# Rows of six experts gathered by quarters of channels and turned by VectorE instead of TensorE

## The chip, the cores and the metric

The kernel runs on one core of a Trainium2 chip. The metric is the time of one execution on the device in microseconds, the median of several executions.

## The reference

A windowed attention (4 batches, 8 heads, 768 positions, 64 channels a head; each query sees the first 8 keys and the last 96) gives 3072 tokens x of 512 channels. A router sends each token to the one expert of eight whose embedding is nearest by cosine, and the expert's output is scaled by the router's probability:

```python
logits = xn @ en.T / tau
expert_idx = np.argmax(logits, axis=1)
...
for e in range(E):
    mask = expert_idx == e
    h = np.maximum(x[mask] @ w1[e], 0.0)           # 512 -> 1024
    out[mask] = gate_w[mask, None] * (h @ w2[e])   # 1024 -> 512
```

All is in fp32. Each expert has 2 MB of w1 and 2 MB of w2. TensorE sums over the 128 partitions, so x must lie with its channels on the partitions (xT) ahead of the first product, while a gather brings tokens onto the partitions (xg).

## The kernel before

The first 200 us are attention and routing; x is written to DRAM (x_dram, one row of 2 KB a token), and so are, for each expert, the numbers of its tokens and their gates (meta, loaded into mt; idss holds the numbers as integers). Then the experts follow one another, each in two parts.

- The arm, one of several code paths by the count w of the expert's tokens (here 320, 512, 320, 352, 384, 480 and 384 for experts 1 to 7), held in a Switch that TensorE, ScalarE (ACT) and VectorE (DVE) enter by a branch. In it `first_by_seven` makes h by Strassen's scheme: seven products of 16 matmuls (L1312) in place of eight, with sums of blocks of w1 (fsum, and one in the place of a block of w1 itself: L1079 to L1082) and of xT (xsum: L1054 to L1057) as operands. The names of these sum lines are shared: `right_sums` and `left_sums` serve several operands, so the operand names tell them apart. After most products `plus` (L1324) adds them up on VectorE, and `fill` then calls a list of pending sums. At the end come the sums of h (hsum) and the rows beyond the first 256 tokens (L1245 for whole tiles of 128, L1258 for pieces of 64 and 32).
- The pair, for the first 256 tokens: seven products again (L1117), with sums of w2 (wsum) and of h. `Pair.begin` and `Pair.end` hold them; `begin` also calls three lists of pending sums.

The sums and the turned rows that expert e+1 needs are made during expert e. `between`, called after each product of the arm, lets TensorE turn one tile of 128 rows of expert e+1 by four transposes (`turn_row`, L1026), and ACT copies the two halves into xT (L1029). In xT the tokens are laced: 16 of one half, 16 of the other. `expert` deals the pending sums to the lists: in the arm the sums of w2, then two of w1 of the next expert, then two of xT; in the pair the other two of xT, then the other two of w1.

The order on every engine is the order of the program text. On POOL, for each e: the gathers of expert e+1 (`gather_rows`, L1000, four of 128 whole rows), then the scatters of the results of expert e-1 (L1264), then a drain. POOL does not enter the arms and so runs ahead: rows of an expert are gathered about a stage before they are turned. On SP's queue, `load_weights` issues w1 of expert e+1 (L167) behind the first product of the pair of expert e-1, and w2 (L168) behind that pair; for expert 2 both wait for the last scatter of expert 0 and come at the start of expert 1. Buffers: two each of w1, w2 and xT, eight tiles xg, four banks for the products.

Of the kernel before, what the change touches and what calls it, by code (L numbers as in the profile page):

```python
# [9 lines left out]
F32 = mybir.dt.float32  # L10
# [10 lines left out]
P = 128  # L21
# [2 lines left out]
PIECES = 32  # L24
FIRST = 256
LACE = 16
WIDTHS = [128] + list(range(160, CAP + 1, 32))
PAIR = WIDTHS.index(256)

# [134 lines left out]

def load_weights(k, e, w):
    nc = k.nc
    first = nc.sync.dma_start(w[0][:], k.w1[e].rearrange("(c p) f -> p c f", p=P))  # L167
    nc.sync.dma_start(w[1][:], k.w2[e].rearrange("(f p) m -> p f m", p=P))  # L168
    return first

# [824 lines left out]
def gather_rows(k, ids, xgp, NJ=CAP // P, upto=None):  # L995

    xgs, issued = [], []
    for j in range(NJ):
        xg = xgp.tile([P, k.DM], F32, name="xg", tag="xg")
        i = k.nc.gpsimd.indirect_dma_start(  # L1000
            out=xg[:], out_offset=None, in_=k.x_dram[0 : upto or k.N + 1, :],
            in_offset=bass.IndirectOffsetOnAxis(ap=ids[:, j, 0:1], axis=0),
        )
        xgs.append(xg)
        issued.append(i.ins)
    return xgs, issued


def new_turned(k):
    return k.xtp.tile([P, k.NC, 2, CAP // 2], F32, name="xT", tag="xT")  # L1010

# [280 lines left out]
            between(f)  # L1292


def first_by_seven(k, now, hT, w, between, spare):


    nc, h = k.nc, w // 2
    a = first_weights(k, now.w[0])
    b = [[now.xT[:, 2 * i : 2 * i + 2, j] for j in range(2)] for i in range(2)]  # L1300
    s1, s2, s3, s4 = now.first_sums
    t1, t2, t3, t4 = now.token_sums
    out = [[laced(hT[:, 4 * i : 4 * i + 4, 0:w])[:, j] for j in range(2)] for i in range(2)]
    number = [0]

    def banks():
        return [k.big.tile([P, CAP], F32, name="big", tag="big") for _ in range(2)]

    def product(to, x, y, add=False):
        for f in range(4):  # L1310
            for l in range(2):
                nc.tensor.matmul(to[f // 2][:, f % 2 * 256 : f % 2 * 256 + h], lhsT=x[:, l, f * P : (f + 1) * P], rhs=y[:, l, 0:h],  # L1312
                                 start=not (add or f % 2 or l), stop=True, skip_group_check=True)
        between(number[0])
        number[0] += 1

    def pairs(ps, q):
        for i in range(2):
            x = ps[i][:].rearrange("p (f n) -> p f n", f=2)[:, :, 0:h].rearrange("p f (q i) -> p f q i", i=LACE)
            yield x, q[:, 2 * i : 2 * i + 2]  # L1320

    def plus(ps, z, q, last=False):
        for (x, to), (_, z) in zip(pairs(ps, q), pairs(ps, z)):
            nc.vector.tensor_tensor(out=to, in0=x, in1=z, op=ALU.add)  # L1324
            if last:
                nc.scalar.activation(to, to, AF.Relu)  # L1326
        fill()

    def fill():
        for make in spare.pop(0):  # L1330
            make()

    (q11, q12), (q21, q22) = out
    fill()
    x, y = banks(), banks()
    product(x, a[0][0], b[0][0])
    for ps, q in pairs(x, q21):
        nc.scalar.copy(out=q, in_=ps)
    product(y, s2, t2)
    plus(y, q21, q12)  # L1340
    product(x, a[0][1], b[1][0], True)
    for ps, q in pairs(x, q11):
        nc.scalar.activation(q, ps, AF.Relu)
    product(y, s3, t3, True)
    plus(y, q21, q22)
    v = banks()
    product(v, s1, t1)
    plus(v, q22, q22, True)
    product(y, a[1][1], t4, True)
    plus(y, q21, q21, True)  # L1350
    product(v, s4, b[1][1], True)
    plus(v, q12, q12, True)


def expert(k, now, coming, widths, unfinished):


    tc = k.tc
    w1, w2 = now.w
    hT = new_hidden(k)  # L1360
    if coming:
        coming.xT = new_turned(k)

    def between(f):
        at = {1: (0,), 2: (1,), 3: (2,), 4: (3,)} if now.e else {5: (0,), 6: (1, 2), 7: (3,)}
        for j in at.get(f, ()) if coming else ():
            turn_row(k, coming.rows, coming.xT, j, k.nc.scalar.copy)

    a = [[hT[:, 4 * j : 4 * j + 4, i * P : (i + 1) * P] for j in range(2)] for i in range(2)]
    now.sums, spare = weight_sums(k, w2)  # L1370
    left, making = hidden_sums(k, a)
    more, ahead = [], []
    if coming:
        coming.token_sums, more = token_sums(k, coming.xT)
        if now.e:
            coming.first_sums, ahead = first_sums(k, coming.w[0])
    spare = [spare[:2], spare[2:], ahead[:1], ahead[1:2], more[:2], []]
    if now.e == 1:
        spare[2:6] = [], ahead[:1], ahead[1:2] + more[:1], more[1:2]
    tiles = range(2 if now.e else 1, CAP // P)  # L1380
    ps = None if now.e else k.work0.tile([P, k.DM], F32, name="work", tag="work")
    k.order = list(range(4, 8)) + list(range(4)) if now.e else list(range(8))
    steps = widths_of(now.e)
    for arm in tc.Switch(now.width.index, len(steps), hint=now.width.hint):
        w = steps[arm]
        if now.e:
            first_by_seven(k, now, hT, w, between, list(spare))
            for make in making:
                make()
        else:  # L1390
            first_by_eight(k, now.xT, w1, hT, w, between)
        for size in (32, 64):
            if w % (2 * size) >= size:
                part_in_arm(k, now, hT, w2, w // (2 * size) * 2 * size, size)
        for j in tiles:
            if j < w // P:
                second_in_arm(k, now, hT, w2, j)
        if ps:
            second(k, ps, hT, w2, range(k.NF // 2))

    def scatters():
        for j in tiles:
            scatter_rows(k, now.y[:, j - 1, :], now.tile_ids[:, j : j + 1])
        for size in (64, 32):
            scatter_rows(k, now.y_part[size][:], now.parts[size][0], P // size)

    def choose_next():
        if coming:
            give_hint(k, coming.e, widths[coming.e])

    out = [scatters]
    if now.e:
        pair = Pair(k, now.rows, a, left, w2, now.sums, not coming)
        choose_next()
        out += unfinished.pop()()
        number = [lambda: widths.append(take_width(k, now.e + 2))] if now.e + 2 < k.E else []
        if now.e == k.E - 2:
            number.append(lambda: load_flag(k))
        if now.e == 2:
            ahead.append(lambda: flag_leftover(k))  # L1420
        pair.begin(spare=(more[2:], number + ahead[2:3], ahead[3:]))
        ps = k.work0.tile([P, k.DM], F32, name="work", tag="work")
        unfinished.append(pair.end(ps[:, 0:256]))
        out.append(pair.scatter(1))
    else:
        choose_next()
        widths.append(take_width(k, 2))
        out += unfinished.pop()()
        for make in more:
            make()  # L1430
        second(k, ps, hT, w2, range(k.NF // 2, k.NF))
        unfinished.append(lambda: end_second(k, now.rows, ps))
    return out
# [172 lines left out]
def kernel(  # L1606
# [40 lines left out]
    with ExitStack() as moe:  # L1647
# [43 lines left out]
        def prepare(e):  # L1691
            t = Net()
            t.e = e
            t.y, t.y_part = ys[e % 2]
            xgs, t.gathers = gather_rows(n, n.ids[:, e], n.xgp)
            t.rows = n.mt[:, e], n.ids[:, e], xgs
            if e < 2:
                t.w = n.w[e]
            else:
                t.w = new_weights(n, (wp_a, n.wp_b)[e % 2])  # L1700
            return t

        with tc.manual_schedule(engines=ORDERED | set(ARMS) | {mybir.EngineType.Pool}):
# [26 lines left out]
            for j in range(CAP // P):  # L1730
                turn_row(n, coming.rows, coming.xT, j, nc.vector.tensor_copy)
            cast(2, n.E)
            split_rows(n, n.mt)
            for y, parts in ys:
                for x in (y, *parts.values()):
# [5 lines left out]
            for e in range(n.E):  # L1741
                now, coming = coming, None
                parts_of(n, now)
                now.width = widths[e]
                if e == 1:
                    now.first_sums = first
                if e + 1 < n.E:
                    coming = prepare(e + 1)
                for scatter in pending:
                    scatter()  # L1750
                if e and coming:
                    wait_for(n, load_weights(n, e + 1, coming.w), [n.outs[-1] if e == 1 else n.out_again])

                nc.gpsimd.drain()
                pending = expert(n, now, coming, widths, unfinished)
# [33 lines left out]
```

## Time and profile before

| | us |
|---|---|
| median of 3 runs (521.31 to 528.96) | 526.16 |
| the profiled execution | 523.85 |
| its span | 522.0 |
| TensorE (PE) busy | 500.9 |
| VectorE (DVE) busy | 301.3 |
| ScalarE (ACT) busy | 197.4 |
| GpSimd (POOL) busy | 148.7 |

The arms of experts 1 to 7 begin at 234.18, 268.58, 320.97, 353.83, 390.62, 429.60 and 479.00 us of the span, their pairs at 254.94, 308.48, 341.55, 377.78, 417.30, 466.80 and 504.10 us.

A line of the timeline gives start, duration (of a run of equal instructions together), engine, line of the kernel, operation, output and inputs with their sizes and the count. A line of the chain of waits gives start, duration and what the chain went through. A line of the table by windows gives the window, its length, the busy time of PE, its weight loads, DVE, ACT and POOL with their counts of instructions, the clock granted to TensorE, the mean busy share of the 16 DMA engines and the GB/s they moved. A group's line gives line, engine, operation, operands and count, then busy us and mean ns of one, then idle time ahead of it and what ended that. "PE x <- y: a, b, c" is a us of waiting in b waits, the longest c.

### The profile page before, as it was taken

How to read it: one execution, taken by the hardware profiler on the slowest of the kernel's cores; microseconds unless marked ns; L12 is line 12 of the kernel's file. 1: busy time of each engine (PE TensorE's matmuls, PEld its weight loads, DVE VectorE, ACT ScalarE, POOL GpSimd, SP SyncE). 2: the span in 40 equal slices, each digit the busy share in tenths (PEclk: the TensorE clock that was granted, in tenths of full speed). 3: DMA queues.
4: the chain of work that ended last, by engine and by line, in shares of the span. 5: the costliest groups of instructions: out<-in, count | busy, mean ns of one | idle time of the engine just before them, and what ended most of it. 6: DMA issues, size and time to landing. Idle time of an engine off the chain costs nothing.

```text
span 522.0 us, 13698 instructions
## 1 busy us (share of the span) xinstructions
PE 500.9 (96%) x5606; PEld 412.8 (79%) x5606; DVE 301.3 (58%) x602; ACT 197.4 (38%) x493; POOL 148.7 (28%) x169
## 2 busy tenths in 40 slices
PE   8999999999987998899989999999999999999995
PEld 7777787787765687859878659989889789859964
DVE  5646667766774664846745606765646644715531
ACT  4966776777644311303222312412312222302210
POOL 4221121432443326253340024153053050013023
PEclk9999999999998999999999999999999999999999
DMA  8989999998524336818682018457066065001001
GB/s 166 202 174 182 220 238 217 222 232 204 131 69 121 104 62 143 251 46 290 207 287 99 2 50 285 156 198 263 3 217 242 4 224 164 1 15 68 0 22 67
DMA packets 111421, 76.32 MB, mean 146 GB/s; under 512 B 87077, under 2 KB 95269, under 8 KB 111281
## 3 DMA queue, kind: packets, MB, share of 16 engines
q1 hardware_dynamic: 102769, 59.00, 42.6%
q0 software_dynamic: 6912, 15.26, 8.7%
q8 instruction: 63, 1.03, 0.9%
q14 instruction: 77, 0.63, 0.5%
q10 hardware_dynamic: 1600, 0.39, 0.3%
HBM read 61.66 MB, written 17.16 MB: 151 GB/s over the span
## 4 chain that ended last, share of the span: by engine, by line
PE 64%; issue 24%; POOL 5%; DVE 3%; ACT 2%; POOLq 1%; DMA 1%; DVEq 0%
PE big L1312 15%; PE big L1117 8%; PE od L512 7%; PE pa L483 6%; PE pa L458 4%; PE work L1258 3%; PE od L522 3%; PE pa L681 3%; PE work L1117 3%; POOL out_dram L1264 3%; PE work L1245 3%; PE work L1026 2%; PE big L1288 2%; PE pa L585 2%; PE work L1036 1%
## 5 line engine op out<-in xcount | busy, mean ns | idle before, releaser
L496 DVE TENSOR_TENSOR ex<-ex,table 126x768 f32<-126x768 f32 x64 | 60.3, 947 | 41.4 <-ACT ex L489 38.5
L1324 DVE TENSOR_TENSOR hT<-big,hT 128x320 f32<-128x320 f32 (+4 forms) x70 | 39.4, 566 | 49.2 <-PE big L1312 46.8
L1264 POOL DMA_INDIRECT out_dram<-y_arm,tids x17 | 17.0, 1002 | 170.4 <-ACT y_arm L1247 121.3
L489 ACT ACTIVATE ex<-pa 126x384 f32<-126x384 f32 (+1 forms) x128 | 53.7, 476 | 24.0 <-PE pa L483 17.7
L1312 PE MATMUL big<-xT,w1t 128*128 128x160 f32 (+4 forms) x336 | 59.4, 330 | 1.3 <-issue 1.3
L1312 PEld LDWEIGHTS big<-xT,w1t 128*128 128x128 f32 x336 | 54.2, 190 | 4.0 <-issue 2.2
L512 PE MATMUL od<-ex,v 126*64 126x192 f32 (+1 forms) x576 | 46.8, 309 | 0.0
L1000 POOL DMA_INDIRECT xg<-x_dram,idss x32 | 32.3, 1011 | 43.9 <-PE big L1312 21.7
L483 PE MATMUL pa<-qT,kT 64*32 64x128 f32 (+3 forms) x2048 | 40.8, 268 | 2.8 <-issue 2.5
L483 PEld LDWEIGHTS pa<-qT,kT 64*32 64x32 f32 (+1 forms) x2048 | 30.5, 107 | 15.2 <-issue 10.6
L512 PEld LDWEIGHTS od<-ex,v 126*64 126x64 f32 x576 | 35.2, 138 | 7.7 <-issue 3.5
L259 POOL DMA_INDIRECT meta<-mt,slot x24 | 27.4, 1141 | 43.8 <-DVE rd L556 17.8
L1312 PE MATMUL big<-xsum,fsum 128*128 128x160 f32 (+4 forms) x224 | 39.6, 330 | 0.0
L1029 ACT COPY xT<-work 128x256 f32<-128x256 f32 x56 | 18.0, 377 | 56.7 <-PE work L1026 55.3
L1312 PEld LDWEIGHTS big<-xsum,fsum 128*128 128x128 f32 x224 | 36.1, 190 | 1.1
L1245 PE MATMUL work<-w2t,hT 128*128 128x512 f32 x80 | 35.1, 593 | 0.0
L1117 PE MATMUL big<-wsum,hsum 128*128 128x256 f32 x136 | 31.1, 380 | 1.5 <-issue 1.0
L1326 ACT ACTIVATE hT<-hT 128x320 f32<-128x320 f32 (+4 forms) x42 | 21.6, 533 | 25.5 <-DVE hT L1324 25.3
L433 POOL COPY v<-v 30x896 f32<-30x896 f32 (+1 forms) x15 | 16.6, 1119 | 49.0 <-DMA v<-in_v_dram 30.5
L1117 PEld LDWEIGHTS big<-wsum,hsum 128*128 128x128 f32 x136 | 25.7, 190 | 6.0 <-issue 1.8
L1245 PEld LDWEIGHTS work<-w2t,hT 128*128 128x128 f32 x80 | 15.1, 190 | 17.7 <-issue 17.6
L1122 DVE TENSOR_TENSOR ptmp<-big,ptmp 128x256 f32<-128x256 f32 x16 | 6.7, 421 | 37.6 <-PE big L1117 16.9
(246 smaller groups left out, 903.0 us busy)
## 6 DMA issues: line engine op xcount, KB each, us to landing
w1t<-in_moe_w_dram SPq DMA_DIRECT2D x6, 2048.0 KB
w2t<-in_moe_w_dram SPq DMA_DIRECT2D x6, 2048.0 KB
v<-in_v_dram SPq DMA_DIRECT2D x32, 192.0 KB
x_dram<-xs SPq DMA_DIRECT2D x23, 256.0 KB
k<-in_k_dram SPq DMA_DIRECT2D x28, 192.0 KB
q<-in_q_dram SPq DMA_DIRECT2D x28, 192.0 KB
w1t<-in_moe_w_dram SPq DMA_DIRECT2D x32, 128.0 KB
w2t<-in_moe_w_dram SPq DMA_DIRECT2D x32, 128.0 KB
```

The costliest lines, as they stand in the source:

```text
L259: i = nc.gpsimd.indirect_dma_start(out=k.meta[:], out_offset=bass.IndirectOffsetOnAxis(ap=slot[:, t : t + 1], axis=0), in_=mt[:, t, :], in ...
L483: i = nc.tensor.matmul(u.sp[e][k0:k1, a * n + c0 : a * n + c1], lhsT=t.kT[rows, j, k0:k1], rhs=t.qT[rows, j * BLK + c0 : j * BLK + c1], st ...
L489: nc.scalar.activation(u.ex[:, e], u.sp[e][0:ROWS, 0 : 2 * u.n].rearrange("p (a c) -> p a c", a=2), AF.Exp, scale=k.scale)
L496: nc.vector.tensor_tensor(out=exv, in0=exv, in1=tab[:, :, 0 : u.n // BLK, :], op=ALU.mult)
L512: nc.tensor.matmul(g.od[a][e * D : (e + 1) * D, at : at + c1 - c0], lhsT=g.v[0:ROWS, 2 * a + e, u.j, :], rhs=u.ex[:, e, a, c0:c1], start=f ...
L1000: i = k.nc.gpsimd.indirect_dma_start(out=xg[:], out_offset=None, in_=k.x_dram[0 : upto or k.N + 1, :], in_offset=bass.IndirectOffsetOnAxis ...
L1117: i = self.k.nc.tensor.matmul(ps, lhsT=x[:, f, :], rhs=w[:, f, :], start=f == 0 and not add, stop=True, skip_group_check=True)
L1245: nc.tensor.matmul(ps[:], lhsT=hT[:, f, j * P : (j + 1) * P], rhs=w2[:, f, :], start=i == 0, stop=i == k.NF - 1)
L1264: i = k.nc.gpsimd.indirect_dma_start(out=k.out.rearrange("t (i m) -> (t i) m", i=n), out_offset=bass.IndirectOffsetOnAxis(ap=ids, axis=0), ...
L1312: nc.tensor.matmul(to[f // 2][:, f % 2 * 256 : f % 2 * 256 + h], lhsT=x[:, l, f * P : (f + 1) * P], rhs=y[:, l, 0:h], start=not (add or f ...
L1324: nc.vector.tensor_tensor(out=to, in0=x, in1=z, op=ALU.add)
L1326: nc.scalar.activation(to, to, AF.Relu)
```

## The change

Experts 2 to 7 get their turned rows another way.

- `gather_quarters`: a tile of 128 tokens is gathered by four indirect DMAs instead of one. Partition 32 b + r of DMA g receives quarter b (128 channels, 512 bytes) of token 32 g + r. The row numbers for it, four times the token's number plus b, are made once for all six experts by `square_rows`, in 16 small VectorE instructions.
- `turn_squares`: one VectorE transpose of 128x512, which turns each square of 32x32 by itself, writes the tile into xT, laced as before. Channels then lie on the partitions as 128 b + 32 c + j on partition 32 b + j, chunk c.
- So w1 of these experts is loaded with its rows in that order, by four DMAs, one for each chunk c.
- `between` stays for expert 0 alone. In experts 1 to 6 the turns take the places in the arm at which two sums of xT stood (one turn in expert 1, two in the others); the others are called at the first place in the pair, all four sums of xT at the second, and the last two sums of w1 at the third.
- Of expert 2, six quarter gathers are issued ahead of the scatters of expert 0, where four whole gathers were, and ten behind them. For the others all 16 stand where the four stood.

```diff
 def load_weights(k, e, w):
-    first = nc.sync.dma_start(w[0][:], k.w1[e].rearrange("(c p) f -> p c f", p=P))
+    src = k.w1[e].rearrange("(b c j) f -> c b j f", b=4, j=SQ)
+    first = [nc.sync.dma_start(w[0][:, c, :], src[c]) for c in range(k.NC)][0]
     nc.sync.dma_start(w[1][:], k.w2[e].rearrange("(f p) m -> p f m", p=P))
...
+def square_rows(k):
+    k.squares = k.tp.tile([P, k.E, CAP // P, 4], I32, name="squares")
+    for b in range(4):
+        for g in range(4):
+            k.nc.vector.tensor_scalar(out=k.squares[b * SQ : (b + 1) * SQ, 2:, :, g], in0=k.mt[g * SQ : (g + 1) * SQ, 2:, :, 0],
+                                      scalar1=4.0, scalar2=float(b), op0=ALU.mult, op1=ALU.add)
+
+def gather_quarters(k, ids, xgs, lo, hi):
+    src = k.x_dram[:, :].rearrange("t (b c) -> (t b) c", b=4)
+    for i in range(lo, hi):
+        j, g = divmod(i, 4)
+        k.nc.gpsimd.indirect_dma_start(
+            out=xgs[j][:, g * P : (g + 1) * P], out_offset=None, in_=src,
+            in_offset=bass.IndirectOffsetOnAxis(ap=ids[:, j, g : g + 1], axis=0),
+        )
+
+def turn_squares(k, xgs, xT, j):
+    half = P // 2
+    k.nc.vector.transpose(
+        out=xT[:, :, :, j * half : (j + 1) * half].rearrange("p c a (g i) -> p g c a i", i=LACE),
+        in_=xgs[j][:].rearrange("p (g c r) -> p g c r", g=4, r=SQ),
+    )
...
     def between(f):
-        at = {1: (0,), 2: (1,), 3: (2,), 4: (3,)} if now.e else {5: (0,), 6: (1, 2), 7: (3,)}
-        for j in at.get(f, ()) if coming else ():
+        for j in {5: (0,), 6: (1, 2), 7: (3,)}.get(f, ()):
             turn_row(k, coming.rows, coming.xT, j, k.nc.scalar.copy)
...
+            turns = [lambda j=j: turn_squares(k, coming.rows[2], coming.xT, j) for j in range(CAP // P)]
-    spare = [spare[:2], spare[2:], ahead[:1], ahead[1:2], more[:2], []]
+    spare = [spare[:2], spare[2:], ahead[:1], ahead[1:2], turns[:1], turns[1:2]]
     if now.e == 1:
-        spare[2:6] = [], ahead[:1], ahead[1:2] + more[:1], more[1:2]
+        spare[2:6] = [], ahead[:1], ahead[1:2], turns[:1]
+    turns = turns[1:] if now.e == 1 else turns[2:]
...
-        pair.begin(spare=(more[2:], number + ahead[2:3], ahead[3:]))
+        pair.begin(spare=(turns, number + more, ahead[2:]))
...
-            xgs, t.gathers = gather_rows(n, n.ids[:, e], n.xgp)
+            if e < 2:
+                xgs, t.gathers = gather_rows(n, n.ids[:, e], n.xgp)
+            else:
+                xgs = [n.xgp.tile([P, n.DM], F32, name="xg", tag="xg") for _ in range(CAP // P)]
+                gather_quarters(n, n.squares[:, e], xgs, 0, 6 if e == 2 else 16)
...
             cast(2, n.E)
+            square_rows(n)
             split_rows(n, n.mt)
...
                 for scatter in pending:
                     scatter()
+                if e == 1:
+                    gather_quarters(n, n.squares[:, 2], coming.rows[2], 6, 16)
                 if e and coming:
                     wait_for(n, load_weights(n, e + 1, coming.w), [n.outs[-1] if e == 1 else n.out_again])
```

More of the change, by code (lines that the diff above doesn't have):

```diff
@@ L26 @@
 LACE = 16
+SQ = 32
 WIDTHS = [128] + list(range(160, CAP + 1, 32))
@@ L1292, in first_by_eight, with first_by_seven @@
             between(f)
-def first_by_seven(k, now, hT, w, between, spare):
+def first_by_seven(k, now, hT, w, spare):
     nc, h = k.nc, w // 2
@@ L1303, in first_by_seven @@
     out = [[laced(hT[:, 4 * i : 4 * i + 4, 0:w])[:, j] for j in range(2)] for i in range(2)]
-    number = [0]
     def banks():
@@ L1313, in product @@
                                  start=not (add or f % 2 or l), stop=True, skip_group_check=True)
-        between(number[0])
-        number[0] += 1
     def pairs(ps, q):
@@ L1371, in expert @@
     left, making = hidden_sums(k, a)
-    more, ahead = [], []
+    more, ahead, turns = [], [], []
     if coming:
@@ L1386, in expert @@
         if now.e:
-            first_by_seven(k, now, hT, w, between, list(spare))
+            first_by_seven(k, now, hT, w, list(spare))
             for make in making:
```

## The prediction

> **What bounds the kernel now.** I read the page first. TensorE is busy for 96% of the span, no other engine for more than 58%.
>
> ```profile
> span 522.0 us, 13698 instructions
> ...
> PE 500.9 (96%) x5606; PEld 412.8 (79%) x5606; DVE 301.3 (58%) x602; ACT 197.4 (38%) x493; POOL 148.7 (28%) x169
> ```
>
> A busy TensorE may still wait inside a matmul's modelled end, so next came the chain of waits and TensorE's own waits from 196 us on. In the experts the chain is TensorE alone: a product of 16 matmuls, four turns of one row tile (L1026, 0.44 us), the next product. All its waits after 196 us sum to some 6 us.
>
> ```profile
> 275.73 0.44 PE work L1026 x4
> 276.16 3.46 PE big L1312 x16
> 279.62 0.44 PE work L1026 x4
> ```
> ```profile
> PE work L1258 <- issue: 1.5, 2, 1.0
> PE big L1312 <- issue: 1.3, 1, 1.3
> ```
>
> So what leaves TensorE's queue shortens the run, as long as nothing else comes to be late. What can come to be late is what feeds it: weights, sums, rows. SP's timeline shows when each expert's w1 (L167) and w2 (L168) are issued, the windows table how fast they flow (last two columns: share of the 16 DMA engines, GB/s), and VectorE's timeline when w1 is first wanted, by the sums L1079 and L1080.
>
> ```profile
> 236.94 0.38 SPq L167 DMA_DIRECT2D w1t<-in_moe_w_dram  x1
> 237.44 0.43 SPq L168 DMA_DIRECT2D w2t<-in_moe_w_dram  x1
> 256.92 0.37 SPq L167 DMA_DIRECT2D w1t<-in_moe_w_dram  x1
> 310.42 0.37 SPq L167 DMA_DIRECT2D w1t<-in_moe_w_dram  x1
> 343.50 0.37 SPq L167 DMA_DIRECT2D w1t<-in_moe_w_dram  x1
> ```
> ```profile
> 257.00:258.00 1.00, 1.00 (x6) 0.89 (x5) 0.00 (x0) 0.00 (x0) 0.92 (x1) 1.00 0.21 17
> 260.00:262.00 2.00, 2.00 (x11) 1.77 (x10) 1.97 (x4) 0.51 (x1) 1.70 (x2) 1.00 1.01 401
> 265.00:266.00 1.00, 1.00 (x6) 0.88 (x5) 0.00 (x0) 0.44 (x1) 0.96 (x1) 1.00 0.17 45
> ```
> ```profile
> 246.97 1.22 DVE L1079 TENSOR_TENSOR fsum<-w1t 128x1024 f32<-128x1024 f32 x1
> 249.58 1.22 DVE L1080 TENSOR_TENSOR w1t<-w1t 128x1024 f32<-128x1024 f32 x1
> 251.24 3.67 PE L1258 MATMUL work<-w2t,hT 128*64 128x256 f32 x32
> 333.60 1.22 DVE L1080 TENSOR_TENSOR w1t<-w1t 128x1024 f32<-128x1024 f32 x1
> 367.56 1.22 DVE L1080 TENSOR_TENSOR w1t<-w1t 128x1024 f32<-128x1024 f32 x1
> ```
>
> The reader is to see: the w1 issued at 256.92 begins to flow 1.2 us later and has landed by 265.2, at 401 GB/s with all engines busy, which is 25 GB/s for each of the 16. And w1 of expert 2, issued at 236.94, is wanted only 10 us later. The others are issued 10.2 to 11.7 us before their stage begins.
>
> [...]Nothing in the trace of before shows a weight load with a narrow outer dimension[...].[...] Its 128x512 sums[...] take 0.69 us.
>
> **The change, part by part.**
>
> Turns leave TensorE. 6 experts x 4 row tiles x 0.44 us = 10.6 us off the chain. The 48 ACT copies (L1029) behind them go as well; ACT is not on the chain.
>
> VectorE gets 24 turns of 128x512. I take 0.69 us each, from the 128x512 sums. Bounds: not below 0.6 (512 elements at the rate of the 128x1024 row, 1.22 us, give 0.6), above perhaps 2.8, if four-byte squares or the output's runs of 16 elements cost four times that. Expert 3 is the tight stage: its VectorE work is 15.35 us in the arm and 6.00 in the pair, with four turns 24.1, with two changes of arm of about 2.8 us (2.6 to 3.2 us of idle time ahead of its first instruction there) 29.7 us; TensorE's stage is 20.58 + 12.28 - 1.75 = 31.1. So 1.4 us is left, and turns are covered up to 1.04 us each. With turns and all four token sums in the pair, VectorE's last instruction there now ends with the pair, where it ended 2.5 us before it (351.34 against 353.83); the next arm's first sums start some 2.5 us later. At the w=320 arm of expert 3 the product sum of L1324 that frees a bank for the fourth product then ends 0.3 us late: 0.4 us of stall. The 16 index instructions (0.17 us each, by L1228's rows of 32 partitions, 2.7 us) stand ahead of memsets and first sums that end at 223.4 while VectorE next waits until 229.2: covered.
>
> ```profile
> 320.97:341.55 20.58, 20.58 (x162) 19.02 (x160) 15.35 (x22) 6.70 (x18) 4.35 (x4) 1.00 0.45 157
> 341.55:353.83 12.28, 12.28 (x58) 10.83 (x59) 6.00 (x10) 2.81 (x6) 6.84 (x6) 1.00 0.65 228
> L1000 POOL DMA_INDIRECT xg<-x_dram,idss x32 | 32.3, 1011 | 43.9 <-PE big L1312 21.7 <-DVE idss L1689 8.5 <-PE work L1026 8.1
> ```
>
> POOL issues 96 quarter gathers for 24 whole ones. One issue every 1.26 us (0.95 and a 0.30 gap) whatever its bytes, since scatters of 128 and 256 columns take 0.98 too. A stage then needs 16 x 1.26 + 6 scatters x 1.4 + 4 (drain and branch) = 32.6 us, against stages of 31 to 50. The scatters queued behind the gathers come up to 13 us later, but their buffers are wanted a stage later, and rows are gathered a whole stage before they are turned. Cost nothing, until an issue takes over 1.9 us.
>
> w1 comes in four DMAs of 512 KB. Their source walks 4 blocks of 32 rows[...], and all four DMAs fall on the same four engines. 2.10 MB at 4 x 25 = 100 GB/s is 21 us, against 5.2. Nearest rows bound it: 5.2 us if the engines are all used after all, 21 if not; I take 21. To this come 1.2 us of start and 1 to 3 us in which gathers and scatters share those engines: 24.5 us from issue. w2 queues behind on those four; it is wanted a stage later.
>
> When it is wanted: L1080 needs all of w1, L1079 its first half. Expert 1: six gathers ahead of the scatters for four, so the last scatter and the w1 behind it come 1.4 us later, at 238.3. Ten late gathers and half of expert 3's lie beside it (3.4 us): it lands at 264. L1080 then ends at 265.5, two product sums (0.98) and a relu (0.47) follow, and TensorE's L1258, in its second half, goes on at 267. Without the delay that half would begin at 251.24 - 1.75 + 1.8 = 251.2. Stall: 15.8 us (12 without sharing, 18 with more). Expert 2: from issue to L1080 11.66 + 18.2 us = 29.8, none. Expert 3: L1080 may start at latest 12.6 us into the stage, 10.55 + 12.6 = 23.1 after issue: 1.4 late (0 to 3). Expert 4: 10.33 + 13.2 = 23.5: 1.0 (0 to 3). Expert 5 has 3.4 us of L1245 between, expert 6 longer products: none.
>
> Sum: -10.6 + 0.4 + 15.8 + 1.4 + 1.0 = +8.0. On the profiled execution's 523.85 us (span 522.0 and 1.85 around it) 531.9. The median of the three runs is 2.3 us above that execution, which gives 534.2; I take 533.
>
> **Rivals.**
>
> B, the load spreads: if the four DMAs use 16 engines, w1 lands as before and only -10.6 + 0.4 is left: 513.7 on the profiled execution, 516 on the median.[...] This is the case in which the chain's reading is the whole story.
>
> C, slow squares, the slower side: VectorE takes the place of TensorE. Price: 2.8 us a turn. Then expert 3's stage is 8.4 us longer on VectorE, 7 beyond TensorE; expert 4's 3.7; expert 5's 1.8; expert 1's lies under the wait for w1. With the forecast's +8 this gives +20: 545. It decides from 1.04 us a turn. For: no such row in the trace, a four-level output.[...]
>
> D, POOL: at 2.5 us for an issue of 512-byte rows a stage needs 52 us, and after 20 us of slack experts 3 to 5 wait for rows: about 540. Against: issues of all sizes take about 1 us.
>
> **How the numbers follow.** Forecast 0.64, B 0.18, C 0.12, D 0.06. The forecast's own range is 526 to 542 (sharing of the four engines, stall of expert 1). About half of it lies above the bound of 2% (10.5 us; that is about what a measurement of this kernel can tell from no change). B lies on that bound: half faster. C and D are slower. Faster 0.09, same 0.42, slower 0.49. The range for 8 in 10 takes in part of B and of C: 517 to 546.
>
> **What would show it.** Right: windows inside 240 to 262 us with a DMA share near 0.25 to 0.4 and about 100 GB/s; VectorE idle ahead of L1080's twin in expert 1 until about 264, ended by a DMA of w1t; TensorE idle some 15 us near 251 to 267; few other waits; turns of 0.7 us. Wrong: w1 at 400 GB/s and no such gap (B); turns over 1 us and VectorE never idle in experts 3 and 4 (C); gaps of POOL's issues over 1.9 us and turns that wait for DMA of xg (D).

## The result and the profile after

The changed kernel took 587.69 us (median of 4 runs, 585.53 to 596.26) against 526.06 for the kernel before: 1.117 times as long, 95% interval 1.106 to 1.128. Some executions of one and the same kernel come out over 1.5% slower than its fastest (596.26 here), and ratios with an interval leave such slow ones out. Forecast were 533, in a range of 517 to 546. Its profiled execution took 586.44 us. The page's first lines:

```profile
span 584.7 us, 13636 instructions
PE 511.0 (87%) x5510; PEld 409.7 (70%) x5510; DVE 319.1 (55%) x642; ACT 183.4 (31%) x445; POOL 218.6 (37%) x241
```

The span grew by 62.7 us. The turns have left TensorE, so it should be busy 500.9 - 10.6 = 490.3 us; it is busy 511.0, 20.7 more. Most of that is the clock: in the stretches after its stops in which the granted clock is 0.50 (some windows below) TensorE is busy for 35.2 us, and half of that, 17.6, is an estimate of what the full clock would have saved. The other 3 us are not accounted for. It is idle for 584.7 - 511.0 = 73.7 us where it was for 21.1, 52.6 more. -10.6 + 20.7 + 52.6 = 62.7.

The moments at which SP issues w2 (L170 now) mark the starts of the stages. From them, expert 1 has become 25.4 us longer, expert 2 0.7, expert 3 15.5, expert 4 15.7, expert 5 5.4, experts 6 and 7 nothing: again 62.7. Forecast were 15.8, 0, 1.4, 1.0 and 0 of stalls. The timeline of SP:

```profile
237.47 5.09 SPq L169 DMA_DIRECT2D w1t<-in_moe_w_dram  x4
242.69 6.12 SPq L170 DMA_DIRECT2D w2t<-in_moe_w_dram  x1
281.18 6.27 SPq L169 DMA_DIRECT2D w1t<-in_moe_w_dram  x4
292.72 0.38 SPq L170 DMA_DIRECT2D w2t<-in_moe_w_dram  x1
```

Next the windows table of expert 1, with the columns as before. w1 flows at about 100 GB/s with a quarter of the DMA engines' time, as forecast (240 to 242: 96 GB/s, a share of 0.28). When w2 has been issued, the engines are full (0.91 to 1.08), yet 232 to 272 GB/s move where the load before reached 401. TensorE stops, and its clock falls to 0.67 and 0.50.

```profile
240.00:242.00 2.00, 2.00 (x17) 2.00 (x16) 1.97 (x4) 0.88 (x2) 1.70 (x2) 1.00 0.28 96
250.00:252.00 2.00, 0.00 (x0) 0.00 (x0) 0.00 (x0) 0.00 (x0) 0.00 (x0) 1.00 0.91 232
252.00:254.00 2.00, 0.00 (x0) 0.00 (x0) 0.40 (x1) 0.00 (x0) 0.00 (x0) 0.67 1.08 272
266.00:268.00 2.00, 0.00 (x0) 0.00 (x0) 0.41 (x1) 0.00 (x0) 1.39 (x3) 0.50 0.44 141
```

The same stretch in the timeline (in brackets the idle time ahead of an instruction and what ended it). VectorE's two sums of w1 both wait, TensorE stops twice behind them, 16.2 us in all, and goes on at 269.78; the prediction had one stop of 15.8 us that ends at 267.

```profile
253.60 1.23 DVE L1110 TENSOR_TENSOR fsum<-w1t 128x1024 f32<-128x1024 f32 x1 [7.56 <-DMA w1t<-in_moe_w_dram]
255.78 3.68 PE L1289 MATMUL work<-w2t,hT 128*64 128x256 f32 x16 [5.92 <-ACT hT L1354]
267.59 1.23 DVE L1111 TENSOR_TENSOR w1t<-w1t 128x1024 f32<-128x1024 f32 x1 [11.97 <-DMA w1t<-in_moe_w_dram]
269.78 2.83 PE L1289 MATMUL work<-w2t,hT 128*64 128x256 f32 x12 [10.32 <-issue]
```

But the wait comes back in experts 3, 4 and 5. VectorE's waits, from 196 us on:

```profile
DVE w1t L1111 <- DMA w1t<-in_moe_w_dram: 32.2, 4, 12.0
DVE fsum L1110 <- DMA w1t<-in_moe_w_dram: 7.6, 1, 7.6
```

TensorE's stops behind w1 come to 30.9 us: 16.2 in expert 1, 4.8, 5.4 and 4.4 in experts 3 to 5. That is the larger part of the 52.6 us of added idle time. Much of the rest are stops that have nothing to do with w1. In expert 3 one stands in the pair: ACT's L1291 has its input by 376.3 and starts at 381.74, and TensorE waits for it. POOL has just ended 16 gathers in a row (358.3 to 380.1):

```profile
376.61 0.94 POOL L1025 DMA_INDIRECT xg<-x_dram,squares  x1 [0.30 <-issue]
379.11 0.95 POOL L1025 DMA_INDIRECT xg<-x_dram,squares  x1 [0.30 <-issue]
381.74 0.47 ACT L1291 ACTIVATE y<-work,pgate 128x256 f32<-128x256 f32 x1 [10.28 <-DMA xg<-x_dram,squares]
382.27 1.98 PE L1148 MATMUL big<-w2t,hT 128*128 128x256 f32 x4 [4.94 <-ACT y L1291]
```

The wait is put down to a gather (DMA xg), but L1291 does not read xg; a name in brackets is inferred. Experts 1 and 2 have such a stop of 4.6 and 3.5 us at the end of POOL's run too. In expert 4 TensorE goes on from 421 to 430 in single steps with gaps (4.8 us in all), while POOL's run lasts from 407.1 to 428.2:

```profile
427.71 0.37 PE L1289 MATMUL work<-w2t,hT 128*32 128x128 f32 x1 [0.98 <-issue]
```

In expert 5, where POOL makes 16 in a row as well, only 0.8 us is lost this way. In the chain of waits POOL's share has grown from 5% of the span, scatters for the most part, to 12%, gathers for the most part. The page's part 4:

```profile
PE 50%; issue 20%; POOL 12%; DMA 10%; DVE 2%; ACT 2%; SPq 1%; POOLq 1%; ACTq 0%; DVEq 0%
```

The two new kinds of instruction themselves take what was forecast (0.69 us a turn, 1.03 us an issue):

```profile
L1025 POOL DMA_INDIRECT xg<-x_dram,squares x96 | 98.7, 1028 | 80.7 <-issue 73.4
L1034 DVE STREAM_TRANSPOSE xT<-xg 128x512 f32<-128x512 f32 x24 | 16.0, 691 | 0.0
```

So 62.7 us, and the 10.6 that the turns should have saved, had to be explained by an edit priced at 18 (the load) and one priced at nothing (the gathers). In what follows "before" is the kernel before on the same chip in the same hour.

### The profile page after: what moved, and what is told of

It reads as the page before. It is cut to its first block, busy times and chain, and to the rows that moved or that the text cites. A ratio compares the mean times of both kernels' runs of the same rounds, so it can differ in the third digit from the quotient of the medians.

```text
span 584.7 us, 13636 instructions
## 1 busy us (share of the span) xinstructions
PE 511.0 (87%) x5510; PEld 409.7 (70%) x5510; DVE 319.1 (55%) x642; ACT 183.4 (31%) x445; POOL 218.6 (37%) x241
## 3 DMA queue, kind: packets, MB, share of 16 engines
q8 instruction: 63, 1.03, 0.8%
## 4 chain that ended last, share of the span: by engine, by line
PE 50%; issue 20%; POOL 12%; DMA 10%; DVE 2%; ACT 2%; SPq 1%; POOLq 1%; ACTq 0%; DVEq 0%
PE big L1342 10%; POOL xg L1025 8%; PE od L514 6%; PE big L1148 6%; DMA w1t<-in_moe_w_dram 5%; PE pa L485 5%; PE work L1276 4%; PE work L1289 3%; PE pa L460 3%; DMA xg<-x_dram,squares 3%; POOL out_dram L1295 3%; PE od L524 3%; PE pa L683 2%; PE work L1148 2%; PE big L1319 2%
## 5 line engine op out<-in xcount | busy, mean ns | idle before, releaser
L1025 POOL DMA_INDIRECT xg<-x_dram,squares x96 | 98.7, 1028 | 80.7 <-issue 73.4
L498 DVE TENSOR_TENSOR ex<-ex,table 126x768 f32<-126x768 f32 x64 | 61.5, 965 | 40.1 <-ACT ex L491 37.3
L1289 PE MATMUL work<-w2t,hT 128*32 128x128 f32 (+1 forms) x320 | 36.4, 408 | 33.7 <-issue 16.5
L1352 DVE TENSOR_TENSOR hT<-big,hT 128x320 f32<-128x320 f32 (+4 forms) x70 | 38.0, 561 | 31.2 <-PE big L1342 22.9
L1289 PEld LDWEIGHTS work<-w2t,hT 128*32 128x32 f32 (+1 forms) x320 | 19.6, 153 | 49.2 <-issue 29.9
L1276 PE MATMUL work<-w2t,hT 128*128 128x512 f32 x80 | 37.4, 621 | 7.9 <-issue 4.9
L485 PEld LDWEIGHTS pa<-qT,kT 64*32 64x32 f32 (+1 forms) x2048 | 30.0, 105 | 14.9 <-issue 10.3
L1148 PE MATMUL big<-w2t,hT 128*128 128x256 f32 x112 | 30.0, 406 | 10.3 <-ACT y L1291 4.9
L1276 PEld LDWEIGHTS work<-w2t,hT 128*128 128x128 f32 x80 | 15.4, 197 | 27.7 <-issue 23.8
```

What stands on the lines that cost most here:

```text
L485: i = nc.tensor.matmul(u.sp[e][k0:k1, a * n + c0 : a * n + c1], lhsT=t.kT[rows, j, k0:k1], rhs=t.qT[rows, j * BLK + c0 : j * BLK + c1], st ...
L498: nc.vector.tensor_tensor(out=exv, in0=exv, in1=tab[:, :, 0 : u.n // BLK, :], op=ALU.mult)
L1025: k.nc.gpsimd.indirect_dma_start(out=xgs[j][:, g * P : (g + 1) * P], out_offset=None, in_=src, in_offset=bass.IndirectOffsetOnAxis(ap=ids[ ...
L1148: i = self.k.nc.tensor.matmul(ps, lhsT=x[:, f, :], rhs=w[:, f, :], start=f == 0 and not add, stop=True, skip_group_check=True)
L1276: nc.tensor.matmul(ps[:], lhsT=hT[:, f, j * P : (j + 1) * P], rhs=w2[:, f, :], start=i == 0, stop=i == k.NF - 1)
L1289: nc.tensor.matmul(ps[i * size : (i + 1) * size, 0:m], lhsT=hT[:, f, base : base + size], rhs=w2[:, f, i * m : (i + 1) * m], start=o == 0, ...
```

## The load of w1

The first theory was that the load is everything. Three kernels give it 16 or 8 engines, and one puts the changed load alone into the kernel before.

`e1_blocks`, the changed kernel with w1 by blocks of 32 partitions:

```diff
-    src = k.w1[e].rearrange("(b c j) f -> c b j f", b=4, j=SQ)
-    first = [nc.sync.dma_start(w[0][:, c, :], src[c]) for c in range(k.NC)][0]
+    src = k.w1[e].rearrange("(b c j) f -> b j c f", b=4, j=SQ)
+    first = [nc.sync.dma_start(w[0][b * SQ : (b + 1) * SQ], src[b]) for b in range(4)][0]
```

> The changed kernel with one edit: w1 is still loaded by four DMAs of 512 KB and in the same order of rows, but each DMA takes one block of 32 partitions with all four chunks, so that the slowest dimension of both sides is 32 and not 4. Theory T (the four DMAs of the change share four of the 16 engines, and all else follows from that): w1 flows near 400 GB/s, VectorE does not wait for it, and the time is 513 to 520 us. Rival R (the quarter gathers, the squares or the new order of the sums make the loss): still above 540 us.

Measured: 576.15 us, before 522.91; 1.094 (1.084 to 1.104). VectorE waits 5.1 us for w1 in all, and yet most of the loss stays. The load is also slower than thought. All engines are full, at half the rate:

```profile
244.00:246.00 2.00, 2.00 (x17) 2.00 (x16) 1.99 (x4) 0.88 (x2) 1.65 (x2) 1.00 1.02 201
```

`e2_before_k4`, the kernel before with the changed kernel's load:

```diff
-    first = nc.sync.dma_start(w[0][:], k.w1[e].rearrange("(c p) f -> p c f", p=P))
+    src = k.w1[e].rearrange("(b c j) f -> c b j f", b=4, j=32)
+    first = [nc.sync.dma_start(w[0][:, c, :], src[c]) for c in range(k.NC)][0]
```

> The kernel before with the changed load of w1 alone. The rows of w1 then stand in another order than those of x, so what experts 2 to 7 compute differs; sizes and order of the work are the same. Theory T: it loses what the changed kernel lost, without the gain of the turns: 585 to 605 us, VectorE's waits for w1t 30 us or more. Rival R: under 550 us.

Measured: 572.07 us; 1.093 (1.087 to 1.100). The load alone costs 49 us. The timeline has VectorE's waits, the windows what flowed:

```profile
256.06 1.23 DVE L1080 TENSOR_TENSOR fsum<-w1t 128x1024 f32<-128x1024 f32 x1 [10.15 <-DMA w1t<-in_moe_w_dram]
267.99 1.23 DVE L1081 TENSOR_TENSOR w1t<-w1t 128x1024 f32<-128x1024 f32 x1 [9.90 <-DMA w1t<-in_moe_w_dram]
365.63 1.23 DVE L1081 TENSOR_TENSOR w1t<-w1t 128x1024 f32<-128x1024 f32 x1 [11.67 <-DMA w1t<-in_moe_w_dram]
```
```profile
338.00:340.00 2.00, 2.00 (x12) 1.74 (x10) 0.56 (x2) 0.75 (x2) 0.97 (x1) 1.00 0.26 105
344.00:346.00 2.00, 2.00 (x17) 2.00 (x16) 1.93 (x2) 0.75 (x2) 0.00 (x0) 1.00 1.00 279
358.00:360.00 2.00, 0.21 (x2) 0.00 (x0) 0.00 (x0) 0.00 (x0) 0.00 (x0) 1.00 0.25 100
```

In expert 3, w1 is issued at 330.69 and VectorE has it at 365.63, 34.9 us later, where the prediction had 24.5. Experts 4 and 5 give 34.2 and 33.6. The trace's packets tell the transfers apart: those of w1 are of 4 KB on SP's queue, those of w2 of 2 KB, and POOL's have a queue of their own. With hardly anything beside it (338 to 340) w1 flows at 100 GB/s on a quarter of the engines' time, so the four engines are as forecast. Two things slow it. POOL's packets share the four engines: in 358 to 360, w1 is only 53 of the 100 GB/s. And while nearly all DMA engines are busy (342 to 356) a packet of w1 takes 0.19 to 0.33 us, where it took 0.16 in 338 to 340: in 344 to 346, beside w2, w1 is 59 of the 279 GB/s.

w2 does not take turns with w1 on the four engines. Of its 1024 packets 768, three quarters, pass from 342 to 352, none from 352 to 362, while w1 is still under way, and the last 256 as w1 ends and after it. The trace does not name a packet's engine, but by these counts the quarter that falls on the four engines queues behind w1, as the prediction had it; it is the rest, on the other engines, beside which w1's packets are slow. Why they are is open.

`e3_b8` and `e4_b16`, the changed kernel with b=8, j=16 and with b=16, j=8 in the source (8 and 16 blocks, rows in another order). In their forecasts k is the number of DMA engines on which w1 is taken to run:

> The changed kernel with w1 walked in 8 blocks of 16 rows instead of 4 of 32, still four DMAs, one for each chunk (the rows of w1 then stand in another order than those of x, so what experts 2 to 7 compute differs). Theory T with k = 8: 200 GB/s, 10.5 us for w1; expert 1 waits a few us, the others not: 514 to 530 us. If not the outermost count but the number of DMAs[...] decides, it stays near 588.

> The same with 16 blocks of 8 rows (order of rows again another, as in the run with 8). Theory T with k = 16: as the run with blocks of 32 partitions, 513 to 520 us. If four DMAs with a mismatched shape are slow by themselves, above 530.

Measured: 584.68 and 595.98 us for 8 blocks, 576.85 and 587.77 for 16. The busy share of the 16 engines rises with the blocks in the source: 0.28 with 4 blocks (240 to 242 of the changed kernel), 0.54 with 8, 1.02 with 16 (a window with w1 under way from each):

```profile
381.00:383.00 2.00, 0.00 (x0) 0.00 (x0) 0.00 (x0) 0.00 (x0) 1.27 (x2) 0.90 0.54 207
269.00:271.00 2.00, 2.00 (x11) 1.77 (x10) 1.59 (x4) 0.51 (x1) 1.39 (x3) 1.00 1.02 268
```

With 8 blocks VectorE's waits for w1 fall from 39.8 us to 13.1, and the time hardly changes. So the theory that the load is everything falls: something else in the changed kernel costs as much.

## The rows and the turns

Four kernels on one chip separate the rest.

`e5_plain`, the changed kernel with w1 in one DMA over all partitions. If a square takes every fourth channel, partition p needs the four rows 4p to 4p + 3 of w1:

```diff
-    src = k.w1[e].rearrange("(b c j) f -> c b j f", b=4, j=SQ)
-    first = [nc.sync.dma_start(w[0][:, c, :], src[c]) for c in range(k.NC)][0]
+    first = nc.sync.dma_start(w[0][:], k.w1[e].rearrange("(p c) f -> p c f", p=P))
...
-        in_=xgs[j][:].rearrange("p (g c r) -> p g c r", g=4, r=SQ),
+        in_=xgs[j][:].rearrange("p (g r c) -> p g c r", g=4, r=SQ),
```

> The changed kernel, with quarter gathers and VectorE turns kept, but w1 in one DMA over all 128 partitions: partition p takes the four rows 4p to 4p+3 (16 KB in one piece), and the turn reads squares with a stride of four channels, so that x lies on the partitions in the same order. Theory L (the load's form is the whole loss; every form tried so far wrote few partitions or used few engines at a time): 511 to 518 us, w1 at about 400 GB/s again, VectorE's waits for w1t under 2 us. Theory G (the quarter gathers, four times as many descriptors and packets, disturb the engines on their own): 540 to 580 us with waits on ACT, VectorE and POOL that no semaphore explains. A strided read of the squares may make a turn longer than 0.69 us; at 1.0 us it would still be covered.

Measured: 568.91 us, before 521.51; 1.092 (1.082 to 1.103). No wait for w1 is left among VectorE's larger waits, and 47 us of loss remain.

`e6_whole`, the same with `gather_rows` for all experts and no `gather_quarters`:

> As the one before, but rows are gathered whole again, four DMAs to an expert in place of 16, at the place where the kernel before had them (rows then lie otherwise on the partitions, so that the turned data are others). Only the turns on VectorE, the sums' new places and the 16 small index instructions are left of the change. Both theories: 511 to 518 us. If it stays above 530 it is the turns or the order of the sums that cost, and both theories fall.

Measured: 516.02 us; 0.990 (0.982 to 0.997). With whole gathers and a good load, the turns on VectorE and the sums' new places together pay 5.5 us, a gain of 0.3 to 1.8%.

`e7_quarters_alone`, the kernel before with `square_rows` and `gather_quarters` in the place of its gathers of experts 2 to 7, `turn_row` and w1 as they were:

> The kernel before, with w1 as it was and rows turned by TensorE, but rows of experts 2 to 7 gathered by quarters (the quarters land on other partitions, so that the data are others). Theory L: 523 to 530 us, the kernel before within its spread. Theory G: 550 to 580 us.

Measured: 574.42 us; 1.102 (1.091 to 1.113). The gathers alone cost 53 us.

`e8_blocks_alone`, the kernel before with the load of `e1_blocks`:

> The kernel before with one edit: w1 in four DMAs of 32 rows of partitions each, all four chunks in each (rows in another order, data otherwise the same). Theory L: a DMA onto only 32 partitions flows at about 200 GB/s with all DMA engines counted busy; w1 lands 6 us later than before, which alone delays expert 1 by about 1 us, but if this form also starves the engines' other traffic the time is 550 to 575 us. Theory G: 523 to 532 us.

Measured: 536.61 us; 1.028 (1.020 to 1.035). This load costs 15 us, not 53 and not nothing; while w1 flows, 205 to 231 GB/s move (240 to 248).

So load and gathers each cost about 50 us alone, and together, with the turns, they make 62. A likely reason is that they stretch the same stages: in expert 3 of the changed kernel TensorE stands and waits for w1 from 364.9 to 369.7, within POOL's run. No run tests it.

## What in the gathers costs

Against whole gathers, quarters are four times the rows and packets, and four times the issues on POOL. `e9_parts` has 16 issues with the old number of rows, `e10_halves` twice the rows and issues, `e11_bits` 12 issues more that move next to nothing, `e12_paused` the full quarters with pauses.

```diff
 e9_parts (kernel before), 16 to an expert
+            out=xgs[j][g * 32 : (g + 1) * 32, :], in_=k.x_dram[0 : k.N + 1, :],
+            in_offset=bass.IndirectOffsetOnAxis(ap=ids[0:32, j, 0:1], axis=0),
 e10_halves (kernel before), 8 to an expert, rows of x_dram as "t (b c) -> (t b) c", b=2
+            out=xgs[j][:, g * 256 : (g + 1) * 256],
+            in_offset=bass.IndirectOffsetOnAxis(ap=ids[:, j, g : g + 1], axis=0),
 e11_bits (kernel before), 12 to an expert behind the four whole gathers, rows as above with b=32
+            out=k.bits[:, i, :],
+            in_offset=bass.IndirectOffsetOnAxis(ap=ids[0:32, 0, 0:1], axis=0),
 e12_paused (e5_plain), in gather_quarters
+        if last is not None and i % 4 == 0:
+            wait_for(k, one, [last])
+        last = one.ins
```

> The kernel before with 16 gathers to an expert in place of four, but each of 32 whole rows of 2 KB: as many issues on POOL as with quarters, as many rows and packets as before (each gather takes the first 32 tokens of its tile again, so that the rows are others). Theory I (a long run of POOL's DMA issues, one behind the other for 20 us and more, holds up the other engines): 550 to 578 us, as with quarters alone, with VectorE and ACT idle until the run ends. Theory R (the four times as many rows and packets of 512 bytes do it): 519 to 528 us.

> The kernel before with eight gathers of half rows (128 of 1 KB each) to an expert: twice the rows and twice the issues (the halves land on other partitions, so that the data are others). Runs of issues of 10 us, with the scatters behind them up to 18. Theory I: 525 to 545 us, since the run is half as long and the engines carry on for the first 10 us or so of a run. Theory R: 535 to 550 us, a third of the added rows with a third of the loss of quarters, or more.

> The kernel before, its four whole gathers kept, with 12 more gathers to an expert of 32 rows of 64 bytes each into a spare tile that nothing reads: 16 issues on POOL, 24 KB more moved. Theory I: 545 to 578 us. Theory R: 519 to 530 us.

> The changed kernel with w1 in one DMA (partition p takes rows 4p to 4p+3) and quarters gathered as before, but each four issues wait until the four before them have landed, so that POOL pauses some 2 us after every 5 us. Theory I: the other engines recover in the pauses, 513 to 535 us against 569 without pauses. Theory R: nothing changes in rows or packets, 555 to 580 us.

Measured, before 521.95: `e9_parts` 593.95 us, 1.135 (1.128 to 1.142); `e10_halves` 526.27, 1.008 (1.004 to 1.012); `e11_bits` 581.12, scattered from 558.34 to 586.01, so no ratio is given; `e12_paused` 535.90, 1.027 (1.022 to 1.033), against 568.91 without pauses. Rows, packets and bytes are not what it takes: 12 small issues of 2 KB each cost 36 us at the least, and 16 issues with the old number of rows 72. It is the issues in a row. `e12_paused` ended just above theory I's range; with its last four gathers and the six scatters it still has runs of ten.

How they cost is seen in the timeline of `e9_parts`, whose POOL issues from 300.0 to 319.3 without a break:

```profile
311.33 0.60 PE L1036 MATMUL work<-ident,xg 128*128 128x128 f32 x4
318.35 0.38 PE L1322 MATMUL big<-xsum,w1t 128*128 128x256 f32 x1 [1.02 <-issue]
318.46 0.86 POOL L1013 DMA_INDIRECT xg<-x_dram,idss  x1 [0.30 <-issue]
321.15 3.20 PE L1322 MATMUL big<-xsum,w1t 128*128 128x256 f32 x6 [0.81 <-issue]
322.58 0.69 DVE L1334 TENSOR_TENSOR hT<-big,hT 128x512 f32<-128x512 f32 x1 [7.71 <-remote]
322.64 1.20 ACT L1039 COPY xT<-work 128x256 f32<-128x256 f32 x4 [12.48 <-remote]
```

ACT's copy has its input at 311.9, from the turn that began at 311.33, and starts at 322.64. TensorE, in the middle of a product, does one matmul every 1.4 us where six take 3.20 later. "remote" is the profile's word for a wait whose end no engine or queue of this core accounts for. The copy's input comes at POOL's tenth issue, and TensorE slows down at the fourteenth. TensorE goes on 1.8 us after the last one ends, VectorE and ACT 3.3 us after it. Summed over TensorE, VectorE and ACT from 225 us on, the "remote" waits are 0 in the kernel before, 0 in `e10_halves`, 73.0 us in `e7_quarters_alone`, 118.7 in `e9_parts`, 9.5 in `e12_paused`, 14.9 in the changed kernel. They are not the whole hold-up: waits like that of L1291 above stand under another name. None of this is to be seen in the profile of before, where POOL makes four to six issues in a row in the experts.

## Closing the two open points

`e13_w2_held` is `e2_before_k4` with w2 held back until w1 has landed:

```diff
-    first = [nc.sync.dma_start(w[0][:, c, :], src[c]) for c in range(k.NC)][0]
-    nc.sync.dma_start(w[1][:], k.w2[e].rearrange("(f p) m -> p f m", p=P))
+    parts = [nc.sync.dma_start(w[0][:, c, :], src[c]) for c in range(k.NC)]
+    first = parts[0]
+    w2 = nc.sync.dma_start(w[1][:], k.w2[e].rearrange("(f p) m -> p f m", p=P))
+    wait_for(k, w2, [i.ins for i in parts])
```

> The kernel before with w1 in the changed kernel's four DMAs (rows in another order), as measured before at 572 us, and one more edit: w2 of the same expert is issued only when all four have landed. If the late landing comes from w2's packets taking turns with w1's on the four engines, w1 lands 24 to 26 us after issue in every stage, VectorE waits for it 12 to 16 us in expert 1 and 1 to 3 in experts 3 to 5 as the prediction had it, and the time is 535 to 545 us. If w2 has no part in it: 565 to 575 us.

Measured: 562.33 us, before 523.74; 1.076 (1.070 to 1.082). So w2's packets cost 10 of the 49 us, and the rest stays. SP's timeline shows w1 issued and, 31.9 us later, w2, that is w1 landed:

```profile
327.00 5.38 SPq L168 DMA_DIRECT2D w1t<-in_moe_w_dram  x4
358.85 0.37 SPq L170 DMA_DIRECT2D w2t<-in_moe_w_dram  x1
```

The other stages give 27.3 to 31.2. The trace's packets account for it. Without w2, w1's 512 packets took 0.186 us each in these 32 us, 23.8 us on four engines. Those of POOL's gathers and scatters took 6.1 us of each engine if they were spread evenly (an estimate), and 1.4 us passed before the first: 31.3. In `e2_before_k4` the same terms for expert 3 are 27.3, 7.3 and 1.4, 36.0 us in all, for 34.9 measured. The prediction had 21 us for w1's packets, 1 to 3 for gathers and scatters, and 1.2.

Three kernels ask what it is about POOL's run. `e14_fills` (kernel before) puts four `memset` of the tile ahead of each whole gather of experts 3 to 7. `e15_bits7` is `e11_bits` with 7 small issues for 12. `e16_paused_all` is `e12_paused` with one more pause, ahead of the scatters.

> The kernel before with four fills of the 128x512 tile on POOL ahead of each of the four whole gathers of experts 3 to 7: a run of 20 instructions on POOL, some 20 us, of which only four are DMA issues. If any long occupation of POOL holds up the other engines: 545 to 575 us. If it is DMA issues alone: 519 to 528 us.

> The kernel before, its four whole gathers kept, with seven more of 32 rows of 64 bytes (11 issues in a run, some 14 us) in place of twelve more. Theory I with a limit near 10 us of a run: 527 to 545 us. If the loss is in proportion to the issues: 22 of 53 us or more, 550 to 557 us.

> The changed kernel with w1 in one DMA and quarters gathered with a pause after every four issues, as measured before at 536 us, and one more pause between the last four gathers and the scatters, so that no run has more than six issues. Theory I: 515 to 527 us; 515 to 520 would be what the turn by VectorE alone gave. If pauses make POOL the bound (some 40 us of it in a stage, against stages of 31 to 50): 530 to 545 us with turns that wait for gathers.

Measured: `e14_fills` 524.64 us, 1.001 (0.999 to 1.004); a POOL that is occupied for 14 us costs nothing. `e15_bits7` 547.30, 1.044 (1.037 to 1.051): a run of the same 14 us, but of 11 issues, costs 24 us, between the two forecasts, and has 23.9 us of "remote" waits. `e16_paused_all` 548.86, scattered from 527.81 to 558.93, so no ratio is given; its trace has no "remote" wait, but POOL is late: the turns wait 14.4 us for gathers.

Last, is it the pace? `e17_spaced_bits` and `e18_spaced_quarters` put four short fills after each issue of `e11_bits` and of `e5_plain`:

```diff
+def space(k):
+    for r in range(4):
+        k.nc.gpsimd.memset(k.pad[:], float(r))
```

> The kernel before with its four whole gathers and 12 more of 32 rows of 64 bytes, as measured before at 581 us, and four short fills of a spare tile on POOL after each of the 16 issues, which should put some 0.6 us between them. If the pace of the issues counts: 520 to 545 us. If it is the number of issues without a landing between: 560 to 585 us, the run being longer still.

> The changed kernel with w1 in one DMA (569 us without a pause) and the same four short fills after each quarter gather. If the pace counts: 515 to 535 us, and below the kernel before if VectorE's turns are then worth what they gave with whole gathers. If it is the number: 560 to 580 us. POOL then needs some 38 us in a stage.

Measured, before 518.05: 551.07 us, 1.059 (1.052 to 1.066), and 542.32, 1.047 (1.043 to 1.051). Both lie between the two forecasts. One issue comes now every 1.8 to 2.4 us, and no "remote" wait is left in either trace, where `e11_bits` had 119.4 us and `e5_plain` 86.7: spacing the issues takes this hold-up away. Whether the pace itself counts, or how many issues have not yet landed, these runs do not separate. What is left is another loss: POOL comes too late. TensorE waits for rows of the whole gathers in `e17_spaced_bits`, 19.3 of 33 us, and VectorE's turns for rows in `e18_spaced_quarters`:

```profile
PE work L1044 <- DMA xg<-x_dram,idss: 19.3, 3, 9.1
```
```profile
DVE xT L1039 <- DMA xg<-x_dram,squares: 19.7, 7, 6.6
```

No version with quarters beat the kernel before. A stage of 31 to 50 us has 22 issues to make; in a row they hold up the other engines, and spread out they come too late. Only `e6_whole` was faster, and its gathers do not deliver what the turn needs.

## Why the prediction was wrong, step by step

- The reading that TensorE bounds the kernel: right, its gaps over 1 us after 225 us sum to 1.3 us. That the chain in the experts is TensorE alone is not quite so: from expert 5 on it goes through POOL's scatters too.
- Turns off TensorE, 10.6 us: 96 instructions are gone from TensorE, as forecast. `e6_whole` shows 5.5 us of gain with them and the sums' new places; in it the turn reads every fourth channel and takes 1.09 us, over the 1.04 up to which the prediction had it covered. What the changed kernel's turn of 0.69 us would give alone was not tried.
- A turn at 0.69 us: 0.691. Rival C is out.
- POOL's pace of 1.26 us: 1.25. But "Cost nothing, until an issue takes over 1.9 us" is the first step that failed, from 0 to 53 us measured alone. It asked whether POOL would be late, and not whether its issues touch anyone else. Rival D had the right engine with a wrong mechanism: issues were not slow, and in the changed kernel turns hardly waited for rows.
- w1 on four engines at 100 GB/s: right, 96 to 100, at a busy share of 0.25 to 0.28 (`e2_before_k4`, 358 to 360; the changed kernel, 240 to 242). That four blocks in the source mean four engines was the author's estimate, which the trace of before did not show; what the runs show is the share, 0.28, 0.54 and 1.02 with 4, 8 and 16 blocks. Rival B is out.
- "24.5 us from issue" is the second step that failed: the 1 to 3 us for sharing. "w2 queues behind on those four" agrees with the counts (the last 256 of w2's 1024 packets passed only as w1 ended and after it), but the prediction took the four engines to run at 25 GB/s each whatever the others do. With the other engines busy, w1's packets took 27.3 us in place of 21, and gathers and scatters some 7 in place of 1 to 3: 34.9 us from issue (`e2_before_k4`, expert 3). In expert 1 the stop came nearly as forecast (16.2 us for 15.8), in part by luck: w1 came 30.1 us after its issue where the prediction had 25.7, and TensorE did half of the rows beyond 256 between two stops. So the number looked safe where it was worked out best. In experts 3 and 4 the prediction had set landing (24.5) against latest use (23.1 and 23.5), a difference of two numbers close together, and expert 5 at nothing: 10 us more of landing became 8.4 to 11.7 us of wait in each of the three in the load alone. 18 us forecast, 49 measured alone, of which w2 beside it makes 10.
- The sum left out that a stop cost twice: after its stops TensorE was busy for 35.2 us at a granted clock of 0.50, by the estimate above 17.6 us more.
- The rival on the slow side was built from one mechanism at 2.8 us a turn and ended at 545. The range took in bounds for the steps that had been priced, but none for the step priced at zero.

## What to carry to other kernels

Count the DMA issues that POOL makes in a row, not their bytes: here eight in a row cost 1%, eleven 4%, sixteen 7 to 13%, though POOL was busy for only 37% of the span in the changed kernel. When a transfer falls on few engines, add what every other queue will put on those engines while it lasts (here some 7 us), allow for a slower pace while the others are busy (here 27.3 us for w1's packets in place of 21), and test every later use of it against the longer landing. An edit priced at zero needs an upper bound like any other.

## What had not been expected of the hardware

- A run of POOL's indirect DMA issues, one every 1.17 to 1.25 us, held up TensorE, ACT and VectorE, in `e9_parts` from the tenth on (eight in a row cost 4 us over the whole kernel, eleven 24). With one every 1.8 to 2.4 us, or a wait for landing after each four, the "remote" waits were gone or down to 9.5 us, and 14 us of fills and four issues on POOL cost nothing (`e14_fills`, 1.001). The loss of a run of 16 varied, in the changed kernel from 0.8 to 4.9 us of TensorE's idle time. What fills up behind POOL is open; the traces show only that waits end late and matmuls come one by one. All times here are of executions recorded by the profiler, so that the hold-up is the same without it is not shown.
- A DMA onto four engines slowed when the others were busy: 0.16 us for a packet of 4 KB in 338 to 340, up to 0.33 in 342 to 356 (`e2_before_k4`); 0.16 to 0.18 in 240 to 250 and 0.25 to 0.28 in 252 to 260 (the changed kernel).
- With DMA engines counted busy all the time, w1 in one DMA moved 401 GB/s (before, 260 to 262); in four DMAs of 32 partitions each 201 to 231 moved (`e1_blocks`, `e8_blocks_alone`). The few partitions are not the whole reason, since `e4_b16` writes all 128 in each of its four DMAs and 231 to 272 moved (268 in 269 to 271). The reason is open.
- The transpose of 128x512 took 0.69 us with squares read from neighbouring elements (the changed kernel) and 1.09 with every fourth (`e5_plain`, `e6_whole`).
- After each of TensorE's seven stops of 4.4 us and more in the changed kernel (from 225 us on) its granted clock went to 0.50, 2.1 to 5.1 us after the stop began, and products after the stop ran at that: TensorE stops at 249.86, and from 252.7 the clock is 0.50. Two stops of 2.1 and 3.0 us, at 353.87 and 322.78, left the clock at 1.00.
